# Attention completed ahead of a turn only for the block that is due, Q/K/V rows stored in halves, attention's first loads issued later

## The chip, the cores and the metric

One Trainium2 chip; the program runs on one of its cores. The metric is the device time of one execution in microseconds (us), the median over runs. The engines are called as in the profile: PE (TensorE, matmuls; PEld its weight loads), DVE (VectorE), ACT (ScalarE), POOL (GpSimd) and SP (SyncE, which here issues nearly all DMAs). Each engine runs its own instructions in order and waits on semaphores for the others.

## The reference

Input x has 2048 rows of 576 numbers. With xn the layer norm of x, the result is x plus two branches that both read xn:

```python
xn  = _layernorm(x, axis=-1)
# branch A: 32 heads of 18; each position looks at 8 earlier ones, 2 apart
q, k, v = split(xn @ wqkv)
idx  = pos[:, None] - (arange(8) * 2)[None, :]
attn = softmax(where(idx >= 0, einsum("bhsd,bhswd->bhsw", q, kg) * 18 ** -0.5, -1e9))
A    = einsum("bhsw,bhswd->bhsd", attn, vg) @ wo
# branch B
h    = relu(xn @ w1 + b1)        # 4608 wide
B    = (h * h) @ w2 + b2
return x + A + B
```

All arithmetic is float32. The kernel makes each float32 product on PE out of a high and a low part (the rounded value, and what rounding left), so most operands are split: ACT writes the high part, DVE the low one.

## The kernel before, in words

**Blocks.** The rows form four blocks b = 0 to 3 of 512 (`TB`); a block's tokens lie four to a partition (`NJ` = 4, index j). The heads form four groups g of eight (`G`), so a group's Q, K and V are 144 columns each (`CG`).

**Rows of Q, K, V.** `qkv_row(b, g, j)` makes 14 matmuls into one bank (L296), and `qkv_out` copies the bank's 432 columns with ACT into the tile `st` (L284). `st` has a single buffer, opened anew at j = 0. After j = 3 `qkv_close` stores K, V and Q with one DMA each to the scratch tensors kscr, vscr, qscr in DRAM (L289). The next group's first copy needs the buffer back, so it waits for the three stores to land.

**Attention.** `attention(b, g)` is a generator of 18 steps, nearly all of them on DVE: four times a product q x K and its reduction (8 steps), the softmax (2 steps, with ACT's exponential at L355), four times a product weights x V and its sums (8 steps). At the end o goes to DRAM (L372). Its inputs come back from the scratch tensors: q (L318) and K, V with a halo (L320), into three buffers `kv`, which `fetch` fills in the order in which `offer` listed the loads, whenever `release` says that one is free. The queue also holds the statistics of a block's rows (`statistics`: mean and scale, `mr`, stored at L146 and read back by `load_mb` as `mb` at L161).

**Who runs it.** `side(k)` takes up to k steps from the current generator, or from the next in the queue whose loads have been issued. `ffn_pair` calls it for 5 steps in a pair, the tile loops of phase B for what `run` has left over, or for 2. `complete(b)` runs whatever is needed before block b's attention is used: as written, first until no (block up to b) is left in the queue, then until nothing at all is current; as `side` goes on to the next in the queue, that empties the queue.

**Order of the program.** All engines but POOL run in the order in which the code is written.
- Opening: `open_rows` normalizes block 0 and makes group 0's rows. `q0` then makes the other rows of blocks 0 and 1, while DVE runs statistics, splits weights and normalizes block 1.
- Phase A0 (`phase_a(0)`): 18 `ffn_pair`s, each 256 hidden columns for blocks 0 and 1 together; block 0's output is summed at once (L483 with `h`, `w2s`), block 1's hidden values are stored to DRAM (L541).
- Turn 0, from pair 17 on: `complete(0)`, then `regroup` fetches o of block 0 with 16 + 16 DMAs (L673), `o_hi` / `o_lo` transpose and split it (L685 to L700), five wo tiles follow the last two w2 tiles, `finish` writes the block out.
- Phase B0 (`phase_b0`): 36 w2 tiles for block 1 from the stored hidden values, with the 32 rows of Q, K, V of blocks 2 and 3 between them; each w2 tile's high part is written by ACT (L456), its low part by DVE (`w2_lo`, into `w2s`), two tiles ahead. At tile 31 come `complete(1)`, both fetches of o (turn 1) and the offers for block 3.
- Phase A1 and turn 2 are like A0 and turn 0 for blocks 2 and 3; phase B1 is a tile loop for block 3 with `side(2)` at each tile, and at tile 22 `complete(3)` and the fetch of o.

Of the kernel before, what the change touches and what calls it, by code (L numbers as in the profile page):

```python
# [8 lines left out]
F32 = mybir.dt.float32  # L9
F32R = mybir.dt.float32r  # L10
BF16 = mybir.dt.bfloat16
AF = mybir.ActivationFunctionType
# [4 lines left out]
P = 128  # L17
S, D, F = 2048, 576, 4608
H, DH, W, DIL = 32, 18, 8, 2
TB = 512  # L20
NB = S // TB
NJ = TB // P
# [5 lines left out]
CG = HG * DH  # L28
# [17 lines left out]
def block_kernel(ctx: ExitStack, tc: tile.TileContext, x, xt, wqkv, wo, w1, b1, w2, b2, out):  # L46
# [231 lines left out]
                mm += [(x4[b][:, js], w[:, 0]), (x4[b][:, js], w[:, 1])]  # L278
        return mm

    def qkv_out(g, j, p):
        if j == 0:
            stage[g] = sb.tile([P, NJ, QW], F32, name="st")
        return nc.scalar.activation(stage[g][:, j], p[:, :QW], AF.Copy)  # L284

    def qkv_close(b, g):
        t = stage.pop(g)
        for i, k in enumerate("kvq"):
            nc.sync.dma_start(scr[k][g][PAD + b * TB:PAD + (b + 1) * TB].rearrange("(p j) c -> p j c", j=NJ),  # L289
                              t[:, :, i * CG:(i + 1) * CG])  # L290

    def qkv_row(b, g, j, i):
        p = bank(i)
        mm = row_products(b, g, j)
        for k, (l, r) in enumerate(mm):
            nc.tensor.matmul(p[:, :QW], l, r, start=k == 0, stop=k == len(mm) - 1)  # L296
        qkv_out(g, j, p)
        if j == NJ - 1:
            qkv_close(b, g)

    def shifted(t, j, *dims):
        a = t[:, j:j + 1, 0:1]
# [70 lines left out]
                release()  # L373
            yield

    current = [None, None]

    def side(k, exp=True):

        while k > 0:  # L380
            if current[0] is None:
                if not queue or queue[0][0] not in landed:
                    return k
                current[:] = [queue.pop(0)[1](), None]
            if current[1] == "exp" and not exp:
                return k
            try:
                current[1] = next(current[0])
                k -= 1
            except StopIteration:  # L390
                current[0] = None
        return 0

    def complete(b):
        while any(n[0] == "k" and n[1] <= b for n, _ in queue):
            assert side(1) == 0
        while current[0] is not None:
            side(1)

    def run(gens, k):  # L400

# [8 lines left out]
    def once(f, *a):  # L410
        f(*a)
        return
        yield
# [330 lines left out]
    def phase_b0():  # L744
        b, r = 1, 0
        todo = [(2 + i, g, j) for g in range(G) for i in range(2) for j in range(NJ)]
        split_up.clear()
        load_xt(3)
        load_wq(0)
        pieces = [normalize(2), once(load_mb, 3), split_wq(0, "S", lambda: load_wq(1)), normalize(3)]  # L750
        open_y(b)
        for n in range(NF):
            w2_hi()
            add(b, tile_products(b, n, hs[0, n // 2]))
            w2_lo()
            if n % 2 and n // 2 + 3 < NP:
                load_h(0, n // 2 + 3)
            run(pieces, 2 if n < 9 else 1)
            while r < 32 and 32 * (n - 6) > 25 * r:
                bb, g, j = todo[r]  # L760
                while bb not in normed or g not in split_up:
                    run(pieces, 1)
                qkv_row(bb, g, j, 2 + r % 3)
                r += 1
                if r == 2:
                    pieces.append(split_wq(1, "w1s", lambda: load_wq(2)))
                if r == 8:
                    pieces.append(split_wq(2, "S", lambda: load_wq(3)))
                if r == 16:
                    pieces.append(split_wq(3, "w1s"))  # L770
                if r == 24:
                    pieces.append(sums(1))
                if j == NJ - 1 and bb == 2:
                    offer(2, g)
                run(pieces, 2)
            if n == 31:
                run_all(pieces)
                last_sum(1)
                complete(1)
                load_w1(NP)  # L780
                load_w1(NP + 1)
                regroup(b, 0)
                regroup(b, 1)
                for g in range(G):
                    offer(3, g)
            if n == 33:
                residual(b)
                combine_w1(NP)
            if n in (33, 34):
                c = 2 * (n - 33)  # L790
                o_hi(b, c), o_hi(b, c + 1)
                o_lo(b, c), o_lo(b, c + 1)
        o_hi(b, 4)
        o_lo(b, 4)
        residual_left(b)
        for c in range(3):
            w2_hi()
            add(b, o_ops(b, c))
            w2_lo()
            if c == 1:  # L800
                w1_hi(NP, 0)
                w1_lo(NP, 0)

        def filler(i):
            if i < 2:
                add(b, o_ops(b, 3 + i), range(NC) if i else ())
            if i == 0:
                w1_hi(NP, 1)
                w1_lo(NP, 1)
            if i == 1:  # L810
                finish(b)

        return filler
# [77 lines left out]
            nc.tensor.matmul(wp[:, :width], warm[:, :P], warm[:, :width], start=True, stop=True)  # L891

    def open_rows():
        xn = sb.tile([P, NJ, NC * P], F32, name="kv", bufs=3)
        open_x(0)
        y = [bank(i) for i in range(5)]
# [80 lines left out]
                part(j, i)  # L977

        def out(j):
            return qkv_out(0, j, qp[j])  # L980

        warm_up(4, TB, x0[:, 0, :1])
        stats(0, 0, 1)
# [68 lines left out]
        xf[0] = sb.tile([P, TB], F32, name="xf")  # L1052
        for j in range(NJ):
            nc.scalar.activation(xf[0][:, j * P:(j + 1) * P], y[left[j]][:, :P], AF.Copy)
        qkv_close(0, 0)

    def q0():
        todo = [(b, g, j) for b, g in ((0, 1), (0, 3), (0, 2), (1, 3), (1, 2), (1, 1), (1, 0)) for j in range(NJ)]
        pieces = [statistics(1), once(load_mb, 1), split_wq(3, "S", lambda: load_wq(2)), normalize(1)]

        def row(r):
            b, g, j = todo[r]
            while b and b not in normed or g not in split_up:
                run(pieces, 1)
            qkv_row(b, g, j, r % 5)
            if j == NJ - 1:
                offer(b, g)
                if not b and g > 1:
                    offer({3: 2, 2: 3}[g])

        for r in range(len(todo) - 2):
            row(r)
            if r == 5:
                pieces.insert(0, split_wq(2, "h", lambda: load_wq(0)))
            if r == 11:
                run_all(pieces)
            if r == 15:
                pieces.append(sums(0))
            if r == 19:
                split_up.discard(0)  # L1080
                pieces.insert(0, split_wq(0, "h"))
            if r == 23:
                run_all(pieces)
                combine_w1(0)
                load_w1(1)
                for n in range(3):
                    load_w2(n)
            if r in (24, 25):
                w1_hi(0, r - 24)
                w1_lo(0, r - 24)  # L1090
            else:
                run(pieces, 3 if r < 4 or 15 <= r < 20 else 2)
# [20 lines left out]
        for k in "kv":  # L1113
            nc.sync.dma_start(scr[k][g][:PAD], zero)
    load_wq(3)
    load_w1(0)
    free[0] = 2
    offer(0, 0)
    filler = q0()
    phase_a(0, filler)  # L1120
    phase_a(1, phase_b0())
# [52 lines left out]
```

## Time and profile before

| | |
|---|---|
| median of 3 runs | 1335.52 us (1333.65 to 1337.85) |
| the profiled execution | 1340.04 us |
| its span, first to last instruction | 1338.3 us |
| busy in the span | PE 1149.0 us (86%), DVE 920.0 us (69%), ACT 572.8 us (43%) |
| mean granted clock of PE | 0.926 of full speed |
| moved by DMA | 254.23 MB, mean 190 GB/s |

Busy times are sums over a whole span in which the stages have different limits; which of them sets the time in a stage has to be read from that stage. A row of the list of waits or a bracket in a timeline names what ended an engine's idle time.

### The profile page before, as it was taken

Reading aid. Unit: us, or ns where it says so; the run is one execution under the profiler, and the core shown is the slowest. Engines: PE = TensorE matmul, PEld = TensorE weight load, DVE = VectorE, ACT = ScalarE, POOL = GpSimd, SP = SyncE. Lnnn points to the kernel's source line nnn. Section 1 sums busy time; section 2 is a strip of 40 time slices with the busy share of each in tenths; the row PEclk is TensorE's granted clock in tenths of the full one; section 3 lists DMA queues with packets and bytes.
Section 4 is the critical chain, followed back from the end, with each engine's and each line's share of the span. In section 5 each row is a group of like instructions: output and inputs, shape, how many; then the busy total and the mean of one; then the engine's idle time right before and its main releaser. Section 6 shows DMA issues by size and latency. Waiting matters only on the chain.

```text
span 1338.3 us, 13583 instructions
## 1 busy us (share of the span) xinstructions
PE 1149.0 (86%) x5013; PEld 956.9 (72%) x5013; DVE 920.0 (69%) x1202; ACT 572.8 (43%) x800; POOL 13.5 (1%) x32
## 2 busy tenths in 40 slices
PE   9397999999999015799989952999999999999978
PEld 7396788888888004588877841688888888878857
DVE  6396797887878994474585773788887877442224
ACT  5222666666665011341321211466667666622212
POOL 2000000000000000000000000000000000000000
PEclk9798999999999558799988975999999999999989
DMA  7555555475663315686757646546454433587764
GB/s 252 203 169 179 177 185 191 149 199 173 163 234 102 145 48 178 230 333 216 251 208 249 223 151 223 163 157 239 142 199 165 143 125 121 181 272 266 246 214 135
DMA packets 106370, 254.23 MB, mean 190 GB/s; under 512 B 29248, under 2 KB 56640, under 8 KB 91712
## 3 DMA queue, kind: packets, MB, share of 16 engines
q1 hardware_dynamic: 106016, 253.00, 56.3%
q8 instruction: 39, 0.64, 0.2%
q10 hardware_dynamic: 288, 0.37, 0.1%
q14 instruction: 27, 0.22, 0.1%
HBM read 191.90 MB, written 61.43 MB: 189 GB/s over the span
## 4 chain that ended last, share of the span: by engine, by line
PE 64%; DVE 15%; DMA 11%; SPq 5%; ACT 2%; issue 2%; DVEq 0%; ACTq 0%
PE p L483 30%; PE p L514 24%; DVE pr L93 7%; PE p L296 4%; PE p L518 4%; SPq L673 3%; DMA qscr<-st 3%; DVE lg L347 2%; DMA h<-h 2%; DMA kv<-kscr 2%; DMA w2r<-in_w 1%; DMA mr<-mr 1%; DVE w2s L93 1%; PE p L973 1%; SPq L289 1%
## 5 line engine op out<-in xcount | busy, mean ns | idle before, releaser
L483 PE MATMUL p<-h,w2s 128*128 128x512 f32 x2010 | 505.1, 401 | 72.1 <-DVE w2s L93 48.5
L483 PEld LDWEIGHTS p<-h,w2s 128*128 128x128 f32 x2010 | 387.6, 194 | 160.8 <-DVE w2s L93 50.7
L514 PE MATMUL p<-X,w1s 128*128 128x512 f32 x864 | 221.4, 392 | 9.4 <-ACT w1s L429 7.8
L514 PE MATMUL p<-S,w1s 128*128 128x512 f32 x648 | 166.9, 393 | 64.5 <-ACT p L548 62.7
L93 DVE TENSOR_TENSOR w2s<-w2r,w2s 128x576 fp32r<-128x576 f32 x164 | 123.4, 755 | 126.0 <-ACT w2s L456 125.6
L514 PEld LDWEIGHTS p<-X,w1s 128*128 128x128 f32 x864 | 162.5, 189 | 45.3 <-ACT w1s L429 8.1
L514 PEld LDWEIGHTS p<-S,w1s 128*128 128x128 f32 x648 | 122.9, 190 | 91.5 <-ACT p L548 63.2
L456 ACT ACTIVATE w2s<-w2r 128x640 fp32r<-128x640 f32 x164 | 119.7, 732 | 147.1 <-PE p L483 110.0
L93 DVE TENSOR_TENSOR pr<-q,kv 128x1152 f32<-128x1152 f32 x64 | 86.8, 1356 | 77.3 <-DMA kv<-kscr 76.1
L93 DVE TENSOR_TENSOR h<-r,h 128x1024 fp32r<-128x1024 f32 (+2 forms) x78 | 93.1, 1198 | 56.6 <-ACT r L529 53.8
L93 DVE TENSOR_TENSOR w1s<-w1r,w1s 128x1024 fp32r<-128x1024 f32 x72 | 88.2, 1225 | 35.4 <-ACT w1s L429 34.4
L521 ACT ACTIVATE r<-r,b1t 128x512 f32<-128x512 f32 x72 | 51.9, 721 | 115.5 <-DVE r L93 115.4
L284 ACT ACTIVATE st<-p 128x432 f32<-128x432 f32 x64 | 32.4, 527 | 133.3 <-DMA qscr<-st 71.6
L93 DVE TENSOR_TENSOR pr<-lg,kv 128x1152 f32<-128x1152 f32 x64 | 86.8, 1356 | 1.5
L347 DVE TENSOR_REDUCE lg<-pr 128x64 f32<-128x1152 f32 x64 | 86.5, 1352 | 1.5
L525 ACT ACTIVATE h<-r 128x1024 fp32r<-128x1024 f32 x72 | 76.1, 1057 | 14.1 <-DMA h<-h 13.0
L93 DVE TENSOR_TENSOR pr<-pr 128x576 f32<-128x576 f32 (+1 forms) x128 | 77.6, 607 | 3.4
L483 PE MATMUL p<-w1s,w2s 128*128 128x512 f32 x260 | 66.9, 417 | 15.3 <-ACT w2s L456 15.2
L429 ACT ACTIVATE w1s<-w1r 128x1024 fp32r<-128x1024 f32 x72 | 75.6, 1050 | 5.2 <-PE p L483 5.2
L529 ACT ACTIVATE r<-r 128x1024 f32<-128x1024 f32 x72 | 76.0, 1055 | 1.2
L483 PEld LDWEIGHTS p<-w1s,w2s 128*128 128x128 f32 x260 | 52.2, 203 | 29.6 <-ACT w2s L456 17.8
L93 DVE TENSOR_TENSOR r<-p,r 128x512 f32<-128x512 f32 (+1 forms) x76 | 52.3, 688 | 27.6 <-ACT r L576 14.8
(124 smaller groups left out, 981.6 us busy)
## 6 DMA issues: line engine op xcount, KB each, us to landing
h<-h SPq DMA_DIRECT2D x72, 1024.0 KB, 5.3
w2r<-in_w SPq DMA_DIRECT2D x144, 320.0 KB, 4.4
w1r<-in_w SPq DMA_DIRECT2D x36, 640.0 KB, 4.0
kv<-kscr SPq DMA_DIRECT2D x16, 1296.0 KB, 5.7
kv<-vscr SPq DMA_DIRECT2D x16, 1296.0 KB, 7.8
r<-in_wqkv SPq DMA_DIRECT2D x16, 432.0 KB, 6.1
w2r<-in_wo SPq DMA_DIRECT2D x20, 320.0 KB, 4.1
w1r<-in_xt SPq DMA_DIRECT2D x6, 1024.0 KB, 5.9
```

Source lines behind the costliest of these rows:

```text
L93: return nc.vector.tensor_tensor(out=out, in0=a, in1=b, op=op)
L296: nc.tensor.matmul(p[:, :QW], l, r, start=k == 0, stop=k == len(mm) - 1)
L347: nc.vector.tensor_reduce(out=lg[:, j * HG:(j + 1) * HG].rearrange("p a w -> p w a"), in_=pr.rearrange("p w (a d) -> p w a d", d=DH), axis ...
L429: nc.scalar.activation(w1s[n, k][:, 0], raw1[n][:, 4 * k:4 * k + 4], AF.Copy)
L456: nc.scalar.activation(w2s[stream[i]][:, :DE], raw2[i], AF.Copy)
L483: nc.tensor.matmul(yp[b][c], v, a, start=c not in yb[b], stop=c in last and c not in [o[0] for o in ops[i + 1:]], skip_group_check=True)
L514: nc.tensor.matmul(to, l, r, start=start and i == 0, stop=i == len(mm) - 1, skip_group_check=True)
L518: nc.tensor.matmul(to, weight(LEFT, k, f), v, start=False, stop=k == 1, skip_group_check=True)
L521: nc.scalar.activation(to, a, AF.Relu, bias=b1t[:, f:f + 1])
L525: nc.scalar.activation(h[:, 0], r, AF.Square)
L529: nc.scalar.activation(r, r, AF.Square)
L673: nc.sync.dma_start(t[g * L:(g + 1) * L].rearrange("l (j i) c -> l i j c", i=G)[:, i], rows[i, :, :, a:z])
```

## The change

Three edits.

1. `complete(b)` runs steps only as long as the queue holds attention of a block up to b, or the current generator is such a one. `current` has a third entry for it, the name. What belongs to later blocks stays where it is.
2. `st` is opened once for a phase (`open_stage`), and `qkv_out` stores K, V and Q after j = 1 and after j = 3, half a block's rows each. A copy into `st[:, j]` now waits for the half store of the group before that reads it. There are 96 stores in place of 48, of half the size.
3. In `q0` the first offers, (0,0) and (0,1), are made after row 5 (r = 5) and no longer before the first row, and w1 is loaded after row 8.

```diff
-    def qkv_out(g, j, p):
-        if j == 0:
-            stage[g] = sb.tile([P, NJ, QW], F32, name="st")
-        return nc.scalar.activation(stage[g][:, j], p[:, :QW], AF.Copy)
-
-    def qkv_close(b, g):
-        t = stage.pop(g)
-        for i, k in enumerate("kvq"):
-            nc.sync.dma_start(scr[k][g][PAD + b * TB:PAD + (b + 1) * TB].rearrange("(p j) c -> p j c", j=NJ),
-                              t[:, :, i * CG:(i + 1) * CG])
+    def open_stage():
+        stage[0] = sb.tile([P, NJ, QW], F32, name="st")
+
+    def qkv_out(b, g, j, p):
+        nc.scalar.activation(stage[0][:, j], p[:, :QW], AF.Copy)
+        if j % 2:
+            for i, k in enumerate("kvq"):
+                nc.sync.dma_start(scr[k][g][PAD + b * TB:PAD + (b + 1) * TB].rearrange("(p j) c -> p j c", j=NJ)[:, j - 1:j + 1],
+                                  stage[0][:, j - 1:j + 1, i * CG:(i + 1) * CG])
...
-                current[:] = [queue.pop(0)[1](), None]
+                name, make = queue.pop(0)
+                current[:] = [make(), None, name]
...
     def complete(b):
-        while any(n[0] == "k" and n[1] <= b for n, _ in queue):
-            assert side(1) == 0
-        while current[0] is not None:
-            side(1)
+        while (any(n[0] == "k" and n[1] <= b for n, _ in queue)
+               or current[0] is not None and current[2][0] == "k" and current[2][1] <= b):
+            left = side(1)
+            assert not left or current[0] is None
...
             if j == NJ - 1:
-                offer(b, g)
-                if not b and g > 1:
-                    offer({3: 2, 2: 3}[g])
+                def go(b=b, g=g):
+                    offer(b, g)
+                    if not b and g > 1:
+                        offer({3: 2, 2: 3}[g])
+
+                if r < 5:
+                    held.append(go)
+                else:
+                    go()
...
             if r == 5:
+                offer(0, 0)
+                for late in held:
+                    late()
+                held.clear()
                 pieces.insert(0, split_wq(2, "h", lambda: load_wq(0)))
+            if r == 8:
+                load_w1(0)
...
     load_wq(3)
-    load_w1(0)
     free[0] = 2
-    offer(0, 0)
     filler = q0()
```

`open_stage()` is called at the head of `open_rows` and of `phase_b0`. PE's order and POOL's are the same as before; what moves stands on SP, DVE and ACT. Three places:

**SP's queue in the opening,** from the last part of a Q/K/V weight load (`r`) to the read of mean and scale (`mr`, `mb`); `kscr_89`, `vscr_93`, `qscr_97` are the scratch tensors of group 0, those one number higher of group 1. Before:

```order
L241 DMA r_404<-in_wqkv 128x432
L419 DMA w1r<-in_w 128x1280
L318 DMA q<-qscr_97 128x576
L320 DMA kv<-kscr_89 128x2592
L320 DMA kv<-vscr_93 128x2592
L146 DMA mr_117<-mr 128x8x1
L161 DMA mb<-mr_117 128x1024
```

With the change:

```order
L241 DMA r_407<-in_wqkv 128x432
L288 DMA kscr_90<-st 128x2x144
L288 DMA vscr_94<-st 128x2x144
L288 DMA qscr_98<-st 128x2x144
L146 DMA mr_117<-mr 128x8x1
L161 DMA mb<-mr_117 128x1024
```

The loads of w1, q, K and V went from ahead of mean and scale to behind them; half of group 1's rows is stored there instead. q, K and V of (0,0) now stand behind the first half store of group 3's rows (`kscr_92` and its like):

```order
L288 DMA kscr_92<-st 128x2x144
L288 DMA vscr_96<-st 128x2x144
L288 DMA qscr_100<-st 128x2x144
L315 DMA q<-qscr_97 128x576
L317 DMA kv<-kscr_89 128x2592
L317 DMA kv<-vscr_93 128x2592
```

They moved past mean and scale, a weight load (three DMAs) and nine half stores.

**DVE at turn 0,** ahead of pair 17 and in it (`pr`, `lg`, `q` belong to attention, `h`, `w2s` and `r` to the pair). Before, within `complete(0)`:

```order
L93 TENSOR_TENSOR pr<-lg,kv 128x1152
L93 TENSOR_TENSOR pr<-pr 128x576
L93 TENSOR_TENSOR pr<-pr 128x288
L93 TENSOR_TENSOR q<-pr 128x144
L93 TENSOR_TENSOR pr<-q,kv 128x1152
L347 TENSOR_REDUCE lg<-pr 128x8x8
```

With the change, in pair 17:

```order
L93 TENSOR_TENSOR h<-r_3348,h 128x1024
L93 TENSOR_TENSOR w2s<-w2r,w2s 128x576 x2
L93 TENSOR_TENSOR r_3506<-p_3436,r_3477 128x512
L93 TENSOR_TENSOR pr<-q,kv 128x1152
L344 TENSOR_REDUCE lg<-pr 128x8x8
L93 TENSOR_TENSOR r_3505<-p_3436,r_3477 128x512
```

Where one attention ended and the next three followed without anything between, the pair's own work stands now, with two steps of attention here and there.

**DVE at the start of phase B1,** behind the output of block 2 (`w2s` is a w2 tile's low half). Before:

```order
L727 SCALAR_TENSOR_TENSOR r_8038<-p_5722,b2t,r_8038 64x512
L93 TENSOR_TENSOR r_8038<-p_5722,r_8038 64x512
L93 TENSOR_TENSOR w2s<-w2r,w2s 128x576 x28
L685 STREAM_TRANSPOSE r_8779<-st 128x512
L93 TENSOR_TENSOR w1s<-r_8779,w1s 128x512
```

With the change:

```order
L93 TENSOR_TENSOR r_7955<-p_5606,r_7955 64x512
L93 TENSOR_TENSOR w2s<-w2r,w2s 128x576
L350 TENSOR_REDUCE mx<-lg 128x32
L93 TENSOR_TENSOR lg<-lg,mx 128x256
L354 TENSOR_REDUCE sm<-lg 128x32
L355 RECIPROCAL sm<-sm 128x32
L93 TENSOR_TENSOR lg<-lg,sm 128x256
L93 TENSOR_TENSOR w2s<-w2r,w2s 128x576
L93 TENSOR_TENSOR pr<-lg,kv 128x1152
L93 TENSOR_TENSOR pr<-pr 128x576
L93 TENSOR_TENSOR pr<-pr 128x288
L93 TENSOR_TENSOR q<-pr 128x144
```

28 low halves in a row were all that DVE had there; now two steps of block 3's attention stand between each two of the first 23.

## Rows read from the trace of the kernel before

**Rows 1.** Stretches: us, busy us of PE PEld DVE ACT POOL, clock, DMA.

```profile
43.70:64.85 21.15, 0.00 (x0) 0.00 (x0) 8.39 (x9) 4.97 (x8) 0.00 (x0) 0.58 0.42 127
429.84:564.24 134.40, 49.13 (x172) 38.14 (x171) 95.28 (x118) 21.97 (x32) 0.00 (x0) 0.67 0.41 143
591.22:775.58 184.36, 172.66 (x786) 152.39 (x784) 124.81 (x149) 44.91 (x75) 0.00 (x0) 0.94 0.68 238
775.58:844.51 68.93, 28.59 (x99) 20.80 (x98) 37.92 (x52) 10.31 (x16) 0.00 (x0) 0.70 0.48 162
1147.45:1187.25 39.80, 39.20 (x173) 31.84 (x171) 17.98 (x25) 19.60 (x27) 0.00 (x0) 1.00 0.72 237
1187.25:1262.94 75.69, 74.23 (x318) 60.77 (x319) 22.81 (x31) 17.80 (x24) 0.00 (x0) 0.98 0.79 260
1262.94:1338.30 75.36, 62.16 (x259) 50.45 (x257) 24.33 (x37) 14.56 (x21) 0.00 (x0) 0.90 0.54 177
```

**Rows 2.** Waits: who for whom, us in total, times, longest.

```profile
DVE pr L93 <- DMA kv<-kscr: 76.1, 4, 28.2
...
PE p L483 <- DVE w2s L93: 48.5, 5, 24.6
```

**Rows 3.** Timeline of SP's queue in turn 0: start, us, what.

```profile
432.28 0.33 SPq L372 DMA_DIRECT2D o<-q  x1
...
458.16 0.32 SPq L372 DMA_DIRECT2D o<-q  x1
```

**Rows 4.** Timeline of SP's queue in the opening.

```profile
30.65 0.52 SPq L146 DMA_DIRECT2D mr<-mr  x1
48.34 0.33 SPq L161 DMA_DIRECT2D mb<-mr  x1
```

**Rows 5.** The tile mr: its three stores and reads.

```profile
DMA to landing us min/median/max: 4.9/10.1/17.7
```

**Rows 6.** Timeline of DVE in the opening, idle time before in brackets.

```profile
54.25 4.88 DVE L93 TENSOR_TENSOR w1r<-w1r,mb 128x1024 f32<-128x1024 f32 x4 [19.85 <-DMA mb<-mr]
...
68.13 1.36 DVE L93 TENSOR_TENSOR pr<-q,kv 128x1152 f32<-128x1152 f32 x1
...
116.85 1.60 DVE L93 TENSOR_TENSOR w1r<-w1r 128x512 f32<-128x512 f32 x3
```

**Rows 7.** Timeline of ACT in the opening.

```profile
63.04 0.95 ACT L284 ACTIVATE st<-p 128x432 f32<-128x432 f32 x2 [1.92 <-DMA qscr<-st]
...
123.67 0.53 ACT L284 ACTIVATE st<-p 128x432 f32<-128x432 f32 x1 [11.16 <-DMA qscr<-st]
```

**Rows 8.** The page's DMA issues: a K load, KB, us to landing.

```profile
kv<-kscr SPq DMA_DIRECT2D x16, 1296.0 KB, 5.7
```

**Rows 9.** Timeline of PE at the end of phase B0.

```profile
796.64 5.64 PE L483 MATMUL p<-h,w2s 128*128 128x512 f32 x14 [12.23 <-DVE w2s L93]
...
826.88 3.35 PE L483 MATMUL p<-h,w2s 128*128 128x512 f32 x7 [24.60 <-DVE w2s L93]
```

**Rows 10.** Timeline of SP's queue at the end of phase B0.

```profile
777.58 0.66 SPq L289 DMA_DIRECT2D qscr<-st  x1
795.94 0.33 SPq L372 DMA_DIRECT2D o<-q  x1
...
797.42 10.66 SPq L673 DMA_DIRECT2D st<-o  x16
808.12 10.22 SPq L673 DMA_DIRECT2D r<-o  x16
```

**Rows 11.** Timeline of DVE at the start of phase B1.

```profile
1192.73 0.74 DVE L93 TENSOR_TENSOR w2s<-w2r,w2s 128x576 fp32r<-128x576 f32 x1
1195.13 0.76 DVE L93 TENSOR_TENSOR w2s<-w2r,w2s 128x576 fp32r<-128x576 f32 x1 [1.65 <-ACT w2s L456]
1198.31 0.76 DVE L93 TENSOR_TENSOR w2s<-w2r,w2s 128x576 fp32r<-128x576 f32 x1 [2.42 <-ACT w2s L456]
```

**Rows 12.** Timeline of SP's queue in phase B1.

```profile
1262.94 13.83 SPq L673 DMA_DIRECT2D st<-o  x16
```

More of the change, by code (lines that the diff above doesn't have):

```diff
@@ L296, in qkv_row @@
             nc.tensor.matmul(p[:, :QW], l, r, start=k == 0, stop=k == len(mm) - 1)
-        qkv_out(g, j, p)
-        if j == NJ - 1:
-            qkv_close(b, g)
+        qkv_out(b, g, j, p)
     def shifted(t, j, *dims):
@@ L374, in attention @@
             yield
-    current = [None, None]
+    current = [None, None, None]
     def side(k, exp=True):
@@ L747, in phase_b0 @@
         split_up.clear()
+        open_stage()
         load_xt(3)
@@ L893, in open_rows @@
     def open_rows():
+        open_stage()
         xn = sb.tile([P, NJ, NC * P], F32, name="kv", bufs=3)
@@ L979, in out @@
         def out(j):
-            return qkv_out(0, j, qp[j])
+            qkv_out(0, 0, j, qp[j])
         warm_up(4, TB, x0[:, 0, :1])
@@ L1054, in open_rows @@
             nc.scalar.activation(xf[0][:, j * P:(j + 1) * P], y[left[j]][:, :P], AF.Copy)
-        qkv_close(0, 0)
     def q0():
@@ L1059, in q0 @@
         pieces = [statistics(1), once(load_mb, 1), split_wq(3, "S", lambda: load_wq(2)), normalize(1)]
+        held = []
         def row(r):
```

## The prediction, made before the changed kernel ran

> **What bounds the kernel now.** I first cut the run into stretches at the turns, the places where a block's attention output is fetched back and multiplied by wo, and read each stretch's busy times [rows 1]. The reader is to see two like stretches that differ: from the last pair of phase A to the first tile of phase B, TensorE (PE) has the same work in both supersteps (172 and 173 matmul records), yet it takes 134.40 us in the first and 39.80 us in the second. In the first, VectorE (DVE) is busy 95.28 us and PE's granted clock is 0.67 (a mean of its two levels, 1.2 and 2.4 GHz: it fell while PE stood); in the second DVE is busy 17.98 us and the clock is 1.00. Other stretches that PE doesn't fill are the wait in the opening (21.15 us without a matmul), the end of phase B0 (28.59 us busy of 68.93) and a part of its rows (172.66 of 184.36 at clock 0.94). Then the list of waits says who is waited for [rows 2]: PE stood 48.5 us in five waits for the low half of a w2 tile (DVE), and DVE itself stood 76.1 us in four waits for a K load. Last come the timelines around these places. In the long pairs of phase A PE has no gap to speak of, so nothing there can be won.
>
> **Turn 0, forecast 89 us won.** SP's row of stored outputs gives the price of one attention when DVE does nothing else: 432.28 to 458.16, 25.9 us [rows 3], for 18 steps, 1.44 us each. Counting `side` steps by the code, `complete(0)` runs 55 of them ahead of pair 17: the rest of (1,3), then (1,2), (1,1), (1,0). None of them is due: block 0's four were done by pair 12. DVE is in order, so ScalarE's copy of pair 17 sits behind it, and PE behind that. The change runs none there (second order piece). What is left is the other turn's 39.80 us [rows 1], which has the same work and an empty queue. So at most 134.4 - 39.8 = 94.6 us are won. Turn 0 also issues, on SP's queue, three loads for block 2 that turn 2 doesn't, and now q and K of (1,1); the last 16 fetches of o stand behind them. A K load lands in 5.7 us [rows 8]; as they overlap with each other and with pair 17 I charge 5 us in all, between 0 (all hidden) and 14 (two and a half in a row). Won: 134.4 - 45 = 89, ends 80 and 95.
>
> **Opening, 11 us won.** PE has nothing from 43.70 to 64.85 [rows 1]: mean and scale of block 1 (`mr`) are issued at 30.65 but land only when SP can go on, at 48.34, 17.7 us later [rows 4]; they stood behind w1, q, K and V of (0,0). The other two such stores landed in 10.1 and 4.9 us [rows 5]. The change puts three half stores ahead instead (first order piece). I take the middle, 10.1: `mr` lands at 40.8, `mb` 5.9 later as now (48.34 to DVE's start at 54.25), so normalizing starts at 46.6, 7.6 us earlier [rows 4, 6]. The copy that held ScalarE 1.92 us for a store also goes free, since its half was stored long before [rows 7]: rows restart 9.5 us earlier. But now K of (0,0) is issued only behind row 5's copy, which ends at 63.99 now, so at 46.6 + 63.99 - 54.25 - 1.92 = 54.4 [rows 6, 7], + 1.8 for three stores, and lands 5.7 us [rows 8] or more later, at 62 to 64, where DVE would be ready at 46.6 + 13.9 = 60.5. So attention starts some 5 us earlier than 68.13, not 7.6, and with it everything up to the combining of w1 at 116.85 [rows 6]. PE's first pair then waited for ScalarE, which stood 11.16 us for a store until 123.67 although DVE was done at 118.45 (116.85 + 1.60) [rows 6, 7]; with halves that wait goes: 5.3 us more. Sum 5 + 5.3, rounded with the earlier restart to 11; ends -3 (K lands no sooner than now) and 18.
>
> **Rows of B0, 16 us won.** Three of the five waits, 48.5 - 12.23 - 24.60 = 11.7 us [rows 2, 9], lie here. DVE takes up (2,g) the moment it is offered, and stands at its K load with the next w2 tile's low half queued behind it. With (1,2) to (2,0) in the queue there is older work, and a K load has a whole half attention (8 steps, 11.5 us) to land. The number of `side` steps here hardly changes (57 to 62 from tile 7 to 30). The clock of 0.94 means some 22 us at half clock; with the waits gone I give back 4 of it. Ends 6 and 20.
>
> **End of B0, 24 us won.** Now `complete(1)` runs 12 steps, so SP issues the last store of o at 795.94, and only behind it 16 + 16 fetches of o, 0.64 us each, until 818.4 [rows 10]; then DVE stands at K of (3,0), issued behind them, and PE for 12.23 and 24.60 us [rows 9]. In the change nothing of block 1 is open at tile 31, so the fetches start when the last half store (issued to 778.2 [rows 10]) has landed, about 781.5: 16 us earlier. They still take 21 us, so PE will still stand about 12 us at the first wo tile and 3 at the second. By my chain the next phase begins at 817 to 825 instead of 844.5; I take 24 of the 20 to 27 us, with 8 as the low end if the fetches remain last.
>
> **Turn 2, 3 us lost.** (3,1) is at work in pair 17. SP's load of V of (3,2) waits for (3,1)'s fourth product, which DVE reaches late in that pair, and 16 fetches of o stand behind it. I charge 3 us, ends 0 and 6.
>
> **B1, 13 us lost.** DVE is nearly idle there now: 22.81 us of 75.69 [rows 1], one low half per 3.18 us tile [rows 11]. Now 46 steps (all of (3,2), (3,3), ten of (3,1)) come in front of block 3's fetches. From 1193.5, behind the low half of 1192.73 [rows 11], this is 46 x 1.44 = 66 us, 22 low halves at 0.7 = 15 and 1 to 2 for two exponentials: 1276, where SP began to fetch at 1262.94 [rows 12]. An iteration costs DVE some 3.6 us against PE's 3.18, so PE falls behind as well. Behind the fetches the rest repeats its 75.36 us [rows 1]. Lost: 13; ends 5 and 22.
>
> **Halves.** 16 more groups of three stores, each about 1.8 us of SP's issue time (0.66 for the last of them [rows 10]); SP waits rather than works, so nothing more is charged.
>
> **Two rules against the change.** The trace shows `mr`, the earliest needed, landing 17.7 us after issue behind loads first used at 68.13 [rows 4, 6]. The Trainium skill, "DMA: Bandwidth & Descriptors", Rules for kernel authors, says to issue a DMA early and wait late; by that, moving these loads back costs up to their 5.7 us instead of winning 11, and the total would be 1228. The trace disagrees here, since early loads held up an earlier need. The same section says to coalesce transfers; with the fixed 2 us that the page's Anatomy of one DMA gives, 48 more stores are an estimate of 96 us if all lay on the path, which makes 1307; no run here shows that fixed part by itself.
>
> **Sum.** -89 - 11 - 16 - 24 + 3 + 13 = -124 us. Against the profiled execution (span 1338.3, 1340.04 with what lies around it) that gives a span of 1214 and 1216 us; that execution stood 4.5 us above the median of the runs shown, 1335.52, so I forecast 1211.5 us.
>
> **Rivals.**
> (a) The end of B0 isn't freed: the 32 fetches, with SP also waiting for the last half stores, end as late as now, and the rows give only 6. For it: SP's issue rate is fixed. Against it: they now start only when 12 steps of DVE are through. -89 - 11 - 6 - 8 + 16 = -98: 1237.
> (b) B1 costs more: DVE's lag delays the fetches by 22 us, and PE's short gaps lower its clock. 1211.5 + 18 = 1230.
> (c) Slower: each deferred attention meets its K load as a round trip. Eleven now run behind turn 0. If each cost PE what the longest did, 24.60 us [rows 9], that is 271 us: 1482. From six such waits on (148 us) the kernel is slower than before. For it: four waits of 76.1 us together exist [rows 2]. Against: all four were attentions taken up as offered or behind the fetches; in phase A0, with a full queue, there is none.
> (d) Every extra store lies on the path: 1211.5 + 48 x 1.8 / 3 = 1240 by SP's issue times.
> (e) The change doesn't do what it says and `complete` still drains: only the opening is won, 1324. The order of DVE speaks against it.
>
> **Chances.** Forecast 0.72 (its own range 1195 to 1229), (a) 0.12, (b) 0.08, (d) 0.04, (c) 0.02, (e) 0.01, no change at all 0.01. A measurement of this kernel tells about 0.3%, 4 us, from no change. Faster 0.97, same 0.01, slower 0.02. The range, 1193 to 1240, takes in (a), (b) and the terms' ends as far as two or three of them fall on one side.
>
> **What would show it.** Right: pair 17 to B0's first tile in 40 to 50 us with no attention on DVE ahead of it; `mr` landing by 41; no wait of DVE for K in B0's rows; fetches at the end of B0 starting within 5 us of the last row's copy; low halves in B1 spaced 3.5 us, and its fetches starting about 89 us behind the first tile, not 75.7. Wrong: PE waiting again for w2's low half in B0's rows, DVE waiting for K more than once or twice, or a turn 0 above 60 us.

## The result, and the profile after

| | before | after |
|---|---|---|
| median | 1336.45 us (4 runs, 1333.65 to 1337.85) | 1219.27 us (4 runs, 1216.85 to 1224.05) |
| the profiled execution, its span | 1340.04, 1338.3 us | 1218.07, 1216.4 us |
| busy PE, DVE, ACT | 1149.0, 920.0, 572.8 us | 1140.7, 916.5, 573.3 us |
| mean granted clock of PE | 0.926 | 0.967 |

The ratio is 0.913, 95% interval 0.910 to 0.916. Forecast were 1211.5 us and 1193 to 1240. Busy times hardly moved: what went is idle time and half clock.

The same stretches as in [rows 1], of the changed kernel (us, busy us of PE PEld DVE ACT POOL, clock, DMA):

```profile
43.50:52.87 9.37, 0.04 (x2) 0.01 (x1) 8.40 (x9) 4.87 (x8) 0.00 (x0) 0.75 0.46 162
423.48:476.95 53.47, 44.84 (x172) 35.55 (x171) 27.32 (x35) 20.80 (x29) 0.00 (x0) 0.87 0.74 251
503.63:668.57 164.94, 164.94 (x785) 147.43 (x784) 132.94 (x161) 45.83 (x76) 0.00 (x0) 1.00 0.76 260
668.57:707.12 38.55, 27.64 (x99) 21.71 (x98) 21.11 (x31) 9.75 (x14) 0.00 (x0) 0.82 0.55 158
1010.07:1060.11 50.04, 42.17 (x172) 34.05 (x171) 25.32 (x32) 20.52 (x29) 0.00 (x0) 0.90 0.72 241
1060.11:1144.79 84.68, 82.24 (x355) 65.46 (x353) 79.91 (x109) 19.52 (x29) 0.00 (x0) 1.00 0.77 285
1144.79:1216.40 71.61, 54.16 (x223) 43.62 (x221) 23.80 (x37) 12.98 (x19) 0.00 (x0) 0.87 0.53 172
```

Row by row: the opening's gap, turn 0, the rows of B0, the end of B0, turn 2, B1 up to block 3's first fetch, and the rest. Turn 0 lost most, and DVE has 35 instructions there instead of 118. In the rows of B0 PE is busy all the time, at full clock. Turn 2 and the first part of B1 grew. Against the forecast, term by term (spans; pair 0 began at 118.13 instead of 125.19):

| place | forecast | measured |
|---|---|---|
| opening, to pair 0 | -11 | -7.1 |
| turn 0 | -89 | 53.47 - 134.40 = -80.9 |
| rows of B0 | -16 | 164.94 - 184.36 = -19.4 |
| end of B0 | -24 | 38.55 - 68.93 = -30.4 |
| turn 2 | +3 | 50.04 - 39.80 = +10.2 |
| B1 | +13 | 156.29 - 151.05 = +5.2 |
| the rest | 0 | +0.4 |
| sum | -124 | -121.9 |

The list of waits of the changed kernel (who for whom, us, times, longest), against [rows 2]:

```profile
ACT st L285 <- DMA qscr<-st: 31.1, 5, 13.6
...
PE p L481 <- ACT w2s L454: 29.7, 7, 7.9
...
PE p L481 <- DMA h<-h: 13.6, 2, 11.4
```

The list names no DVE wait for a K load any more, and no PE wait for a low half among the long ones. (In the opening DVE still stood 5.54 us before the first attention at 61.65, which the list calls "issue"; K of (0,0), issued at 54.03, landed 7.5 us later, just before.) PE now waits for ACT's high part of a w2 tile (at the turns, where ACT itself waits behind o) and for stored hidden values (in B1).

### The profile page after: what moved, and what is told of

Its sections match the earlier page's. It is cut to its first block, busy times and chain, and to the rows that moved or that the text cites. A ratio compares the mean times of both kernels' runs of the same rounds, so it can differ in the third digit from the quotient of the medians.

```text
span 1216.4 us, 13713 instructions
## 1 busy us (share of the span) xinstructions
PE 1140.7 (94%) x5013; PEld 950.8 (78%) x5013; DVE 916.5 (75%) x1202; ACT 573.3 (47%) x800; POOL 13.5 (1%) x32
## 4 chain that ended last, share of the span: by engine, by line
PE 75%; DMA 8%; DVE 8%; SPq 5%; issue 2%; ACT 2%; POOL 0%; DVEq 0%; ACTq 0%; POOLq 0%
PE p L481 31%; PE p L512 26%; PE p L295 12%; PE p L516 5%; SPq L671 4%; DMA h<-h 3%; DVE pr L93 3%; DVE w2s L93 2%; DMA w2r<-in_wo 1%; DMA w2r<-in_w 1%; DMA mr<-mr 1%; DMA qscr<-st 1%; ACT w2s L454 1%; PE p L973 1%; DVE w1r L93 1%
## 5 line engine op out<-in xcount | busy, mean ns | idle before, releaser
L481 PE MATMUL p<-h,w2s 128*128 128x512 f32 x2010 | 492.1, 393 | 16.7 <-DMA h<-h 13.6
L481 PEld LDWEIGHTS p<-h,w2s 128*128 128x128 f32 x2010 | 378.8, 189 | 102.3 <-issue 14.3
L512 PEld LDWEIGHTS p<-X,w1s 128*128 128x128 f32 x864 | 162.5, 189 | 49.3 <-ACT w1s L427 12.2
L481 PE MATMUL p<-w1s,w2s 128*128 128x512 f32 x260 | 73.9, 450 | 27.4 <-ACT w2s L454 27.4
L481 PEld LDWEIGHTS p<-w1s,w2s 128*128 128x128 f32 x260 | 57.7, 224 | 43.0 <-ACT w2s L454 29.8
L427 ACT ACTIVATE w1s<-w1r 128x1024 fp32r<-128x1024 f32 x72 | 75.7, 1051 | 2.0 <-PE p L481 1.9
L516 PE MATMUL p<-x,w1s 128*128 128x512 f32 x216 | 66.5, 389 | 0.0
```

The costliest lines, as they stand in the source:

```text
L427: nc.scalar.activation(w1s[n, k][:, 0], raw1[n][:, 4 * k:4 * k + 4], AF.Copy)
L481: nc.tensor.matmul(yp[b][c], v, a, start=c not in yb[b], stop=c in last and c not in [o[0] for o in ops[i + 1:]], skip_group_check=True)
L512: nc.tensor.matmul(to, l, r, start=start and i == 0, stop=i == len(mm) - 1, skip_group_check=True)
L516: nc.tensor.matmul(to, weight(LEFT, k, f), v, start=False, stop=k == 1, skip_group_check=True)
```

## Experiments

All times are medians of four runs; each ratio is to the kernel before, run on the same chip. A table of the stretches of these kernels stands behind the first four.

**1. The first edit undone** (`undo_complete`):

```diff
-        while (any(n[0] == "k" and n[1] <= b for n, _ in queue)
-               or current[0] is not None and current[2][0] == "k" and current[2][1] <= b):
-            left = side(1)
-            assert not left or current[0] is None
+        while any(n[0] == "k" and n[1] <= b for n, _ in queue):
+            assert side(1) == 0
+        while current[0] is not None:
+            side(1)
```

> The changed kernel (1219.3 us) with the first edit undone: complete empties the whole queue again; halves and late first loads stay. The theory, that this edit alone made turn 0, the rows of B0 and the end of B0 shorter (81, 19 and 30 us between the two profiles) and turn 2 and B1 longer (10 and 5), expects 1219 + 81 + 19 + 30 - 10 - 5 = about 1334 us, with turn 0 above 130 us again. The rival, that the 19 us of B0's rows came from the half stores (ScalarE's waits for a store fell from 71.6 to 31.1 us), expects 1315 us and rows of B0 in about 165 us.

Measured: 1325.1 us, 0.992 (0.990 to 0.995); turn 0 takes 134.5 us again.

**2. The first edit alone**, in the kernel before (`only_complete`; the diff is the one above the other way round, with the third entry of `current`).

> The kernel before (1336.5 us) with the first edit alone. The theory expects everything but the opening's 7 us: 1226 us, turn 0 about 53 us, rows of B0 about 165 us. The rival (the half stores made B0's rows shorter) expects 1245 us and rows of B0 near 184 us.

Measured: 1229.6 us, 0.922 (0.919 to 0.924).

**3. The third edit undone** (`undo_late`):

```diff
-                if r < 5:
-                    held.append(go)
-                else:
-                    go()
+                go()
...
-            if r == 8:
-                load_w1(0)
...
+    load_w1(0)
     free[0] = 2
+    offer(0, 0)
```

> The changed kernel with the third edit undone: q, K, V of the first attentions and w1 are loaded ahead of mean and scale again. The theory (these loads hold up mean and scale) expects pair 0 at about 125 us instead of 118 and 1226 us in all, with mean and scale read at about 48 us instead of 39. The rival, the rule to issue loads early, expects the first attention sooner and no loss: 1219 us or less.

Measured: 1220.5 us, 0.914 (0.912 to 0.916).

**4. The second edit undone** (`undo_halves`):

```diff
-        if j % 2:
+        if j == NJ - 1 and (b or g):
+            qkv_close(b, g)
```

`qkv_close` is that of the kernel before, and `st` is opened anew at j = 0.

> The changed kernel with the second edit undone: Q, K, V of a block's rows are stored after the fourth row again, in one store each. The theory that halves do little expects 1219 to 1224 us, the difference in the opening alone, where ScalarE waits for a store. The rival expects 1238 us, with the rows of B0 near 184 us.

Measured: 1227.8 us, 0.920 (0.918 to 0.922).

Stretches in us, from the profiles (A0 is pair 0 to pair 17):

| | pair 0 at | A0 | turn 0 | B0 rows | end of B0 | turn 2 | B1 |
|---|---|---|---|---|---|---|---|
| before | 125.19 | 304.65 | 134.40 | 184.36 | 68.93 | 39.80 | 151.05 |
| changed | 118.13 | 305.35 | 53.47 | 164.94 | 38.55 | 50.04 | 156.29 |
| undo_complete | 119.46 | - | - | 177.78 | 70.64 | - | 147.76 |
| only_complete | 124.16 | 305.92 | 53.98 | 169.47 | 41.26 | - | 155.93 |
| undo_late | 121.27 | - | - | 164.95 | 38.67 | - | 156.10 |
| undo_halves | 119.36 | - | - | 166.68 | 44.05 | - | 156.09 |

The first edit alone wins 106 us, the other two together 10.5, all three 116 to 117: they add up. Turn 0 belongs to the first edit alone (53.98 us with it and nothing else). The rows of B0 are shared: 169.47 with the first edit alone and 177.78 without it. So both forecasts of experiments 1 and 2 gave the first edit some 4 to 9 us too much, and the rival's share is real but small.

Undoing the halves costs 8.5 us, more than the theory's 0 to 5 and less than the rival's 19. Of it 1.7 us lie in the rows of B0 and 5.5 at its end. ACT's timeline in B0 with whole stores shows why (idle time in brackets; two of its seven waits of 3.8 to 15.5 us for a store in these rows), and SP's at the end of B0:

```profile
603.67 0.53 ACT L287 ACTIVATE st<-p 128x432 f32<-128x432 f32 x1 [15.54 <-DMA qscr<-st]
...
623.30 0.53 ACT L287 ACTIVATE st<-p 128x432 f32<-128x432 f32 x1 [7.91 <-DMA qscr<-st]
```

```profile
676.73 0.68 SPq L293 DMA_DIRECT2D qscr<-st  x1
677.46 2.08 SPq L422 DMA_DIRECT2D w1r<-in_w  x2
681.34 11.27 SPq L676 DMA_DIRECT2D st<-o  x16
```

ACT stands for the stores of the group before, while the w2 tiles' high parts queue behind it; with halves ACT has no wait for a store in these rows. At the end the fetches start 9.2 us behind the last row (672.14), not 3.9, and PE waits 10.17 us instead of 6.79. I had weighed the rule of the Trainium skill to coalesce many small transfers ("DMA: Bandwidth & Descriptors", Rules for kernel authors), and priced the 48 more stores at 2 us each. The Trainium skill gives that fixed part (the same page, Anatomy of one DMA) for DMAs that GpSimd issues; these are SP's. Here the finer stores win 8.5 us, since what counts is when the buffer is free again; this trace goes against coalescing them. The run undoes the half stores and the single opening of `st` together, so the share of each is not shown.

The third edit is worth 1.2 us, less than can be told. With the loads early, `mr` is late as before (read at 48.29 us) and PE's rows restart at 62.09 instead of 52.87; but of these 9.2 us only 3.1 are left at pair 0, which comes at 121.27 where the theory expected 125. The time is nearer to the rival's. Experiment 8 shows what else pair 0 waits for.

**5. No loads of attention between the fetches of o** (`hold`), and **6. the first hidden values behind the fetch as well** (`hold_h`):

```diff
-        while free[0] and loads:
+        while free[0] and loads and not hold[0]:
...
                 complete(b)
+                hold[0] = 1
                 regroup(b, 0)
...
-        load_h(s, 0)
         next(end)
         regroup(b, 1)
+        load_h(s, 0)
+        hold[0] = 0
+        fetch()
```

`load_h` moves in experiment 6 only. While `hold` is set, `side` takes up no attention whose V isn't loaded.

> The changed kernel (1219.3 us), in which no load of attention (q, K, V) is issued between the two fetches of o in turns 0 and 2; they follow behind the second fetch. The theory, that turn 0 lost its 13.7 us over turn 2 of before because the second fetch stood on SP's queue behind q of the next attention, which waited 8.3 us for a store of o to land, and turn 2 its 10.2 us partly behind a V load, expects turn 0 in 43 to 45 us instead of 53.5, turn 2 in 44 to 47 instead of 50.0, and about 1206 us. The rival, that the fetches themselves run slowly because other transfers share the DMA engines (17.4 us for the 16 of turn 0 against 10 to 11 elsewhere), expects turn 0 above 50 us and 1216 us or more.

Measured: 1219.0 us, 0.914 (0.913 to 0.916): the rival's time. Turn 0 takes 49.2 us, 4.3 less than in the changed kernel, but B0's first tiles take 2.0 and B1 1.5 us more, and turn 2 is no shorter (50.2 us).

> The same, and the first load of hidden values for the next phase, which waits for their last store to land, goes behind the second fetch of o as well. The theory, that whatever waits on SP's queue ahead of the fetch delays it by as much, expects 3 to 5 us less in each turn than the kernel with the held loads alone: about 1199 us. The rival: the next phase's first tile then waits for these hidden values, and nothing or less than nothing is won.

Measured: 1213.7 us, 0.910 (0.909 to 0.912), less than experiment 5 on the same chip. SP's queue in turn 0, of the changed kernel, of experiment 5 and of experiment 6:

```profile
428.91 0.39 SPq L369 DMA_DIRECT2D o<-q  x1
437.23 0.32 SPq L315 DMA_DIRECT2D q<-qscr  x1
...
441.35 0.33 SPq L740 DMA_DIRECT2D h<-h  x1
441.73 17.42 SPq L671 DMA_DIRECT2D r<-o  x16
```

```profile
429.00 0.42 SPq L541 DMA_DIRECT2D h<-h  x1
...
439.90 0.33 SPq L745 DMA_DIRECT2D h<-h  x1
440.28 11.55 SPq L676 DMA_DIRECT2D r<-o  x16
```

```profile
432.58 16.13 SPq L676 DMA_DIRECT2D r<-o  x16
```

In the changed kernel q of (1,1) waits 7.8 us for the store of o, and the second fetch stands behind it. With that gone, SP waits 6.9 us for the last store of hidden values instead, and the fetch starts only 1 us earlier after pair 17's first matmul (17.2 us instead of 18.3). With that gone too it starts another 7 us earlier (9.9) and then takes 16.1 us instead of 11.6, so it ends 2.7 us earlier than in experiment 5. Yet turn 0 is no shorter for it (49.3 us); PE then waits there for ACT's high parts, at most 3.48 us at a time. What experiment 6 wins over experiment 5 lies later: 2.5 us in turn 2 (47.7), 1.6 in A1 and 0.9 in B1. Both theories had half: waits in a row on the queue, each hiding the next, and behind them fetches that go out slowly (the last section shows why).

**7. Attention's DMAs on POOL's queue** (`pool`):

```diff
-                nc.sync.dma_start(q.rearrange("p j c -> p (j c)"),
+                nc.gpsimd.dma_start(q.rearrange("p j c -> p (j c)"),
...
-                nc.sync.dma_start(oscr[b, g].rearrange("(p j) c -> p j c", j=NJ), q)
+                nc.gpsimd.dma_start(oscr[b, g].rearrange("(p j) c -> p j c", j=NJ), q)
```

(and the K and V loads alike). One more thing differs: POOL runs its own instructions in the order in which they are written from `q0` on (`tc.manual_schedule`).

> The changed kernel with the loads of q, K, V and the stores of o issued by POOL, which has little else to do, and no longer by SP. The theory, that the waits of these DMAs hold up others behind them on SP's queue, expects all of it gone: in the opening no wait of ScalarE of 11 to 14 us for a half store, and pair 0 at about 112 us instead of 118; turn 0 in 43 to 47 us and turn 2 in 43 to 47; about 1200 us. The rival, that the DMA engines and not the queue are what is short there, expects 1215 to 1220 us. Unknown is what POOL takes to issue such a DMA; the trace shows it.

Measured: 1212.3 us, 0.909 (0.908 to 0.911), between the theory and its rival: pair 0 at 115.04, ACT's longest wait for a half store in the opening 6.78 us, turn 0 48.8 us, turn 2 50.1. What it showed best was not asked for. POOL issues K and V of (0,0) as soon as group 0's rows are stored, and `mr` is late again. POOL's timeline, then SP's:

```profile
28.56 0.54 POOL L317 DMA_DIRECT2D kv<-kscr  x1
29.09 0.54 POOL L317 DMA_DIRECT2D kv<-vscr  x1
```

```profile
29.48 0.64 SPq L146 DMA_DIRECT2D mr<-mr  x1
47.86 0.33 SPq L161 DMA_DIRECT2D mb<-mr  x1
```

SP's queue holds no attention load ahead of `mr`, and `mr` still lands after 18.4 us, as in the kernel before (17.7 us [rows 4]) and unlike the changed kernel (29.34 to 39.36, 10.0 us). So transfers in flight with it are enough to make `mr` late; it need not stand behind them on SP's queue.

The Trainium skill, "DMA: Bandwidth & Descriptors", section "Issuing engines are not separate DMA queues", gives a ground for this: whatever engine starts them, DMAs run on the same 16 engines and interleave. The trace agrees, as loads that POOL issued hold up SP's `mr` (18.4 us). The Trainium skill adds there that several issuers save only the time to initiate, usually little. Here POOL takes 0.54 us to issue such a DMA, no less than SP (mostly 0.3 to 0.55); what it takes off SP are the waits ahead of these DMAs.

**8. The first offers after row 9** (`late9`):

```diff
-                if r < 5:
+                if r < 9:
                     held.append(go)
...
-            if r == 5:
+            if r == 9:
                 offer(0, 0)
...
+            if r == 5:
                 pieces.insert(0, split_wq(2, "h", lambda: load_wq(0)))
```

> The changed kernel (1219.3 us) with the first offers of attention made after row 9 and no longer after row 5, so that q, K and V of (0,0) are loaded behind five more groups of half stores. The theory, that these loads (1.3 MB each for K and V) share the DMA engines with whatever small store is in flight, and that the third edit only moved them from mean and scale onto the half stores (ScalarE stands 11.7 us for one at 73.7 us), expects that wait below 5 us and pair 0 at 110 to 114 us instead of 118, with nothing changed behind it: 1212 to 1215 us. The rival: what pair 0 waits for is VectorE's chain to w1 and the store that it meets at 116.6 us (13.6 us), which stand as they are, and pair 0 stays at 118 or comes later.

Measured: 1218.7 us, 0.914 (0.912 to 0.916): no change, where 1212 to 1215 us were expected; pair 0 at 115.42. ACT's timeline in the opening, of the changed kernel and of experiment 8:

```profile
73.68 0.95 ACT L285 ACTIVATE st<-p 128x432 f32<-128x432 f32 x2 [11.74 <-DMA qscr<-st]
...
116.60 0.53 ACT L285 ACTIVATE st<-p 128x432 f32<-128x432 f32 x1 [13.60 <-DMA qscr<-st]
117.03 1.05 ACT L427 ACTIVATE w1s<-w1r 128x1024 fp32r<-128x1024 f32 x1
```

```profile
103.99 0.95 ACT L285 ACTIVATE st<-p 128x432 f32<-128x432 f32 x2 [0.18 <-DMA qscr<-st]
...
114.31 1.06 ACT L427 ACTIVATE w1s<-w1r 128x1024 fp32r<-128x1024 f32 x1 [6.88 <-DVE w1r L93]
```

Both waits go, as the theory said, but pair 0 gains 2.7 us, not 4 to 8: then ACT waits for DVE's w1. And A0 takes 2.0 us more, so nothing is left; why A0 does is open. The rule of the Trainium skill to issue early and wait late ("DMA: Bandwidth & Descriptors", Rules for kernel authors), which the prediction weighed, is neither borne out nor refuted by the time: offers before row 0, after row 5 and after row 9 give 1220.5, 1219.3 and 1218.7 us.

**9. One more step of attention in each pair of A1** (`more_a1`):

```diff
-        side(2, False)
+        side(3 if s else 2, False)
         work(3)
```

> The changed kernel with one more step of attention in each pair of phase A1, so that 17 of the 46 steps in front of block 3's fetches in B1 are done before. The theory, that these 46 steps cost B1 8.5 us (156.3 us against 147.8 with complete undone), expects B1 in about 148 us, A1 unchanged, 1211 us. The rival, that VectorE (busy 253.5 of A1's 303 us) holds up the pairs of A1 instead, expects A1 longer by 10 us or more and 1219 us or more.

Measured: 1206.8 us, 0.905 (0.904 to 0.906): faster than the changed kernel. B1 takes 145.88 us, and A1 with its turn only 0.8 us more (DVE busy 282.4 of A1's 303 us). PE's longest wait in B1, of the changed kernel and of experiment 9:

```profile
1165.42 12.43 PE L481 MATMUL p<-h,w2s 128*128 128x512 f32 x42 [11.39 <-DMA h<-h]
```

```profile
1155.06 12.27 PE L481 MATMUL p<-h,w2s 128*128 128x512 f32 x42 [5.53 <-DMA h<-h]
```

The fetches begin 72.3 us behind the first tile instead of 84.7, and the hidden values behind them on the queue come earlier.

**10 to 12. Together.** `best_a` is 6 and 9. `best_b` also spreads block 3's fetches over eight tiles; `best_c` is `best_b` with POOL's queue (all but (0,0), and POOL's own order as in experiment 7) in place of the held loads.

```diff
-            if n == 22:
+            if n == 17:
                 complete(b)
-                regroup(b, 0)
+            if 17 <= n < 25:
+                regroup(b, (n - 17) // G, [(n - 17) % G])
...
-            if n == 25:
-                regroup(b, 1)
```

> The changed kernel with two of the edits tried before: one more step of attention in each pair of A1 (12.5 us won alone), and no load of attention or of hidden values between the two fetches of o (5.5 us won alone). If the two places are independent: 1201 us. If they hide each other: 1206 us.

> The same, and in B1 the 32 fetches of o of block 3 are spread over eight tiles, four at a tile from tile 17 on, as attention is through by then. The theory, that the 16 fetches in a row hold up the loads of w2 and of hidden values behind them on SP's queue (PE stood 5.5 and 2.3 us there in the kernel with one more step, and 11.4 and 2.0 in the changed kernel), expects these waits gone and B1 in about 138 us instead of 146: 1193 us. The rival, that it is bandwidth, expects the waits to stay at other tiles: 1201 us.

> The kernel with the spread fetches, but loads of q, K, V and stores of o issued by POOL (those of (0,0) excepted, which stay on SP behind mean and scale), and no loads held back. The theory, that a store of o waiting for VectorE, and q waiting for that store, hold up the half stores behind them in the opening (ScalarE's 13.6 us), expects pair 0 at 110 to 113 us instead of 118, and with the turns as short as with the loads held: 1187 us. The rival, that the K and V loads delay the half stores as much from another queue, expects pair 0 at 115 us or later and 1193 us.

Measured: 1206.4 us, 0.904 (0.902 to 0.907); 1199.8 us, 0.899 (0.897 to 0.902); 1195.0 us, 0.897 (0.894 to 0.900). The held loads add nothing to experiment 9: the time is the 1206 us named for places that hide each other, but what the trace shows is another reason, since the turn before B0 gets 4.3 us shorter while the first tiles of B0 take 1.8 and B1 2.6 us more; why B1 does is open. Spreading wins: B1 takes 139.86 us (expected 138), though from 1206 us this gives 1199.8 and not 1193. Of the wait for hidden values this is left:

```profile
1150.99 6.63 PE L483 MATMUL p<-h,w2s 128*128 128x512 f32 x28 [2.31 <-DMA h<-h]
1158.47 12.96 PE L483 MATMUL p<-h,w2s 128*128 128x512 f32 x56 [0.85 <-DMA h<-h]
```

In `best_c` pair 0 came at 117.34, not at 110 to 113: its rival's case, and ACT again waits for DVE's w1 (6.35 us). Its turn 2 is short (25.7 us from the last w1 product to B1, 34.4 in the changed kernel), but its end of B0 is 6 us longer, in a profiled run that was the longest of its four (1200.75 us). `best_b` and `best_c` can't be told apart; both beat the changed kernel, by some 1.5 to 1.8%.

## Why the prediction was right, and where its steps failed

**The main mechanism held.** `complete(0)` ran work that was not due, and without it turn 0 fell by 80.9 us; the end of B0 and its rows gave 50 more. Experiments 1 and 2 show that the first edit is the cause: 106 of 117 us.

**Turn 0, 8 us too much.** The step that failed is the charge of 5 us for SP's queue; turn 0 took 53.47 - 39.80 = 13.7 us more than the turn it was measured by, the high end named (14). Its 53.47 us also lie above the 40 to 50 us that I had named as a sign of being right. I had priced a K load by its landing time. What held SP was q of (1,1), which waits until o of (1,3), just ended, has landed from the same buffer; behind it, hidden by it, the wait for the last store of hidden values; then fetches at 1.09 us each (17.42 / 16) instead of 0.64 (experiments 5 and 6).

**Opening, 4 us too much.** `mr` at 39.36 (said 40.8), the normalizing at 44.29 (46.6), PE's rows at 52.87 (55.3) and attention at 61.65 (62 to 64) came as said or earlier. The step that failed is "with halves that wait goes": ACT stood 11.74 and 13.60 us for half stores. That `mr` came as said has some luck in it: I had read 10.1 and 4.9 us in [rows 5] as its two other stores, but they are the median and the least of six DMAs, three of them reads. The page of before has 12.1 us as the median of the three stores. And its place behind those loads on the queue is not needed to make it late: that they are in flight is enough (experiment 7). Moved back, they met the half stores instead (experiment 8), and behind these waits stands DVE's chain to w1.

**Rows of B0, 3 us too little.** No DVE wait for K is left, as said; full clock gave the rest. A part of what I had put down wholly to the first edit comes from the other two (169.47 us without them against 164.94).

**End of B0, 6 us too little.** The fetches started at 672.42, 3.1 us behind the last row's copy (within 5, as said), and took 21.5 us. I had kept 12 and 3 us of PE's waits; the profile of the changed kernel shows

```profile
688.26 5.78 PE L481 MATMUL p<-w1s,w2s 128*128 128x512 f32 x14 [6.79 <-ACT w2s L454]
698.16 9.12 PE L481 MATMUL p<-w1s,w2s 128*128 128x512 f32 x28 [4.12 <-ACT w2s L454]
```

as the first wo tiles need only the first 16 fetches. The step that failed is the 12 us kept for the first wo tile: it cost 6.79, and 10.17 with whole stores. So 2.7 us of the place (41.26 with the first edit alone) to 5.5 us (44.05 with the halves undone) are the halves'.

**Turn 2, 7 us too little.** SP's queue there, and PE:

```profile
1023.34 0.33 SPq L317 DMA_DIRECT2D kv<-vscr  x1
1028.41 0.33 SPq L740 DMA_DIRECT2D h<-h  x1
1028.79 12.94 SPq L671 DMA_DIRECT2D r<-o  x16
```

```profile
1045.57 14.71 PE L481 MATMUL p<-w1s,w2s 128*128 128x512 f32 x51 [7.87 <-ACT w2s L454]
```

The V load that I named held SP 1.8 us. The step that failed is to charge that load alone. What I had not counted is q and K of (3,2), in flight with the first 16 fetches (15.54 us instead of 10.19), and the store of hidden values, which came later and took 8.7 us to land instead of 4.8: SP stood 4.7 us for it.

**B1, 8 us too much.** DVE's pace was right, a low half every 3.3 to 3.6 us:

```profile
1070.51 0.75 DVE L93 TENSOR_TENSOR w2s<-w2r,w2s 128x576 fp32r<-128x576 f32 x1
...
1074.07 0.75 DVE L93 TENSOR_TENSOR w2s<-w2r,w2s 128x576 fp32r<-128x576 f32 x1
...
1084.53 0.75 DVE L93 TENSOR_TENSOR w2s<-w2r,w2s 128x576 fp32r<-128x576 f32 x1
...
1087.85 0.75 DVE L93 TENSOR_TENSOR w2s<-w2r,w2s 128x576 fp32r<-128x576 f32 x1
```

The fetches came 84.7 us behind the first tile (said 89; before 75.7). The step that failed is "the rest repeats its 75.36 us": PE did not stand meanwhile. It had 355 matmuls behind it by then, not 318, so less was left (71.61 us). That is 4 of the 8 us; the fetches' coming earlier than said is the other 4. That deferred attention is what delays the fetches is shown by experiment 9.

The errors cancel, by luck: +8, +4 and +7 us against -3, -6 and -8, so that the sum missed by 2 us. Most of the 7.8 us between 1211.5 and 1219.3 comes from elsewhere: I had taken off 4.5 us because the profiled execution before stood that far above its median, and the one after stood 1.2 us below its own. The time was right to 0.6%, better than its terms.

## What to carry to other kernels

Before a block is used, finish what that block needs and nothing else, and then place the deferred work where the engine has room: here one step more per pair in a phase with idle DVE time won another 12 us. On an in-order DMA queue list everything that waits ahead of an urgent transfer; taking out the first wait shows the next, so price the whole row of them. And a transfer can be late through its place on the queue or through what is in flight with it; moving a DMA to another queue tells the two apart.

## What the runs showed of the hardware

**A small store is slowed by big loads from another queue.** `mr` (4 KB) took 10.0 us to land behind a weight load and three half stores, and 18.4 us behind the same with K and V loads (1.3 MB each) that POOL had issued at 28.56 and 29.09 (experiment 7).

**SP's issue of small DMAs follows the landing of earlier, unrelated ones.** The waits of SP's queue in the changed kernel:

```profile
SPq L671 <- DMA h<-h: 13.8, 6, 3.2
...
SPq L288 <- DMA kv<-kscr: 5.2, 2, 3.4
...
SPq L671 <- DMA kv<-kscr: 3.8, 2, 2.6
```

The fetches of o (L671) need neither, and the half stores (L288) need no K load. The program gives SP's DMAs eight semaphores in turn, and in the trace a DMA waits on its own before it is issued, that is until the eighth DMA before it has landed. Three of the 16 fetches of turn 0 show it:

```profile
445.10 0.54 SPq L671 DMA_DIRECT2D r<-o  x1
...
447.69 0.54 SPq L671 DMA_DIRECT2D r<-o  x1
...
453.48 0.54 SPq L671 DMA_DIRECT2D r<-o  x1
```

The eighth DMA before each is K, issued at 437.60 and landed 7.5 us later; the store of hidden values (438.12, 9.6 us); and their load (441.35, 12.1 us). So 16 fetches of 24 KB take 10.22 us on a quiet queue (683.70, end of B0), and 11.55 to 17.42 us with larger transfers among the eight.

**POOL as issuer** took about 0.54 us for such a DMA, and K landed in 8.8 us (median) instead of 7.4 from SP; why is not shown.
